# Threshold attention and mixer on one core: half of the weight tiles of six pairs transposed by TensorE, the DMA engines in the planner's model, last-row sums through SyncE's queue

## The chip, the core and the metric

The kernel runs on one core of one Trainium2 chip. A core has five engines with an instruction queue each: TensorE (PE, with its weight loads shown apart as PEld), VectorE (DVE), ScalarE (ACT), GpSimd (POOL) and SyncE (SP, which here only issues DMAs). They meet through semaphores. Sixteen DMA engines move data for all queues. The metric is the device time of one execution in microseconds (us).

## What is computed

The reference, cut to what matters (8 batches, 8 heads, 576 rows, head size 64; model size 512, hidden size 2048, rank 32):

```python
scores = scale * np.matmul(q, k.transpose(0, 1, 3, 2))
thresh = np.max(scores, axis=-1, keepdims=True) - tau
scores = np.where(scores >= thresh, scores, -1000000000.0)
scores = scores - np.max(scores, axis=-1, keepdims=True)
attn = np.exp(scores)
attn = attn / (np.sum(attn, axis=-1, keepdims=True) + 1e-09)
a = np.matmul(attn, v)                      # per batch and head
x = a.transpose(0, 2, 1, 3).reshape(B, S, H * D)
h = x.transpose(0, 2, 1) @ U @ V            # low-rank mixing of the rows
u = x + h.transpose(0, 2, 1)
out = u + np.maximum(u @ w_ch1, 0.0) @ w_ch2
```

Everything comes and goes as float32.

## The kernel before, in words

**Pairs and steps.** The 64 heads are taken as 32 pairs of two heads (four pairs a batch). A pair has five score steps, one for each tile of 128 rows of its 576 rows, so there are 160 steps; the fifth tile has 64 rows for each head, and both heads share one tile of 128 partitions. Per pair the work is:

- twelve loads of q, k and v issued by GpSimd (L271), two pairs ahead; TensorE turns q and k (L315, L330) and ScalarE copies them out (L323, L338);
- per step the scores by TensorE into the two PSUM tiles `scores0` and `scores1` (L380; L387 for the fifth), one for each head. VectorE negates and stores them with their row minimum (L400), ScalarE makes the threshold (L412) and the exponentials (L419), VectorE selects and multiplies (L427), which leaves a weight tile in one of eight buffers `w_ring` and the row sums in `d_ring`. The next step's scores wait for both L400 of the step before;
- the transpose of every weight tile by a DMA that SyncE issues (L441, eight in a pair; L444, two of half size for the fifth tile), from `w_ring` into `wT`. A buffer of `w_ring` is used again by the eighth tile after;
- the last-row sums: the sums of the fifth tile's second head lie on other partitions than the reciprocal needs, and GpSimd moves them by one tiny DMA in even batches (L457) and by two, the second waiting for the first, in odd ones (L459, L460). VectorE then takes the reciprocals (`rec`, L495 and L497);
- the product with v by TensorE (L476, two halves of 20 matmuls, called AV here), which waits for all of the pair's `wT`; the copy out (L489), the turn back (L504 to L508, called back), the scaling into `x` by VectorE (L521, L525), the low-rank product (L544, L559, L562), the sum u (L570, L574) and the turn of u (L594, L598).

After four pairs the batch has its mixer: 32 groups of four matmuls with W1 (L637, called p1 here), the ReLU on ScalarE (L647), 8 to 10 groups of eight matmuls with W2 (L663), the final sum (L676) and the stores (L689 to L693). W1 and W2 come in sixteen DMAs by GpSimd (L720, L723), one released at every second score step from the seventh on.

**The order.** Class `Order` writes the program. Each piece of work is a task with an engine, a cost in us, tasks that it waits for, and a number of the four shared PSUM banks. `run` keeps a clock for each engine and again and again takes the task that can start first; of those of one engine that could start within 0.15 us of the first, it takes the one whose `rank` is lowest (time when it was ready plus its `off`, and for the mixer a due step `when`). A task with a `lag` counts as done that long after its engine is free: 3.0 us for a load, 2.5 us for the sums, 4.5 us for a transpose in the first eight pairs and 2.8 us later. Where TensorE would wait over 0.45 us by this clock, it puts in matmuls on a constant tile (`fill`, L218), 0.22 us each. On the chip each engine runs its list in the written order and waits at whatever is not ready.

## Time and profile before

| | |
|---|---|
| median of 3 runs | 708.54 us (706.43 to 714.72) |
| the profiled execution, its own time | 708.51 us |
| its span, first to last instruction | 706.7 us |
| mean granted TensorE clock | 0.982 |
| busy | PE 677.4 us, DVE 513.1, ACT 480.3, POOL 377.5 |
| moved by DMA | 90.29 MB in 220172 packets |

How to read the views: the page gives each engine's busy time and, in 40 equal slices, its busy tenths, with the granted clock (PEclk) and the mean busy share of the sixteen DMA engines. The windows view gives the same for chosen stretches, the busy us of PE, PEld, DVE, ACT and POOL with the number of instructions behind each, then clock, DMA share (over 1 where several packets of an engine overlap) and GB/s. A row of the timeline is: start, duration, engine, line, operation, output and input, shapes, count, and in brackets the idle time of that engine just before and what ended it. Matmuls overlap, so the time from one start to the next is a little less than the duration.

### The profile page before, as it was taken

The page shows a single profiled execution, that of the slowest core. Times are in us where ns is not written, and L with a number is a line of the kernel's source. Part 1 is how long each engine was busy: PE and PEld are TensorE (multiplying, and loading weights), DVE is VectorE, ACT ScalarE, POOL GpSimd, SP SyncE. Part 2 cuts the span into 40 slices and gives each one's busy share as a digit, 9 for nine tenths or more (in the row PEclk, how much of TensorE's full clock was granted, in tenths as well). Part 3 has the DMA queues.
Part 4 walks back from the last instruction along what each step waited for, and adds up shares of the span by engine and source line. Part 5 has one row for each costly group of instructions (what it writes and reads, how often), then busy time and mean ns, then how long its engine had stood idle before and what let it go on. Part 6 is the DMA issues. An engine that isn't in the chain of part 4 may idle for free. (4 is left out here: it accounts for less than half of the span.)

```text
span 706.7 us, 15090 instructions
## 1 busy us (share of the span) xinstructions
PE 677.4 (96%) x5172; PEld 412.7 (58%) x5172; DVE 513.1 (73%) x1371; ACT 480.3 (68%) x1106; POOL 377.5 (53%) x591
## 2 busy tenths in 40 slices
PE   9997998879999999999999999999999999999994
PEld 4454555546666666656666666656666665656662
DVE  4889697568788879678788879678788878683201
ACT  5567575657778777767778777767777777765540
POOL 9967738466665466646655466646655461211111
PEclk9999998989999999999999999999999999999998
DMA  6899999978777777677776777677867775461212
GB/s 140 164 154 157 166 169 186 168 125 141 120 145 128 133 138 143 129 148 117 133 144 129 132 136 148 124 139 110 162 135 128 133 137 94 86 115 34 45 30 45
DMA packets 220172, 90.29 MB, mean 128 GB/s; under 512 B 205632, under 2 KB 210704, under 8 KB 220096
## 3 DMA queue, kind: packets, MB, share of 16 engines
q1 hardware_dynamic: 195504, 47.46, 43.7%
q0 software_dynamic: 23712, 41.66, 29.1%
q8 instruction: 41, 0.67, 0.4%
q10 hardware_dynamic: 880, 0.21, 0.1%
q14 instruction: 35, 0.29, 0.1%
HBM read 36.86 MB, written 9.44 MB: 66 GB/s over the span
## 5 line engine op out<-in xcount | busy, mean ns | idle before, releaser
L419 ACT ACTIVATE e_sb<-s_sb,m 128x576 bf16<-128x576 f32 x288 | 220.7, 766 | 71.2 <-DVE s_sb L400 69.1
L427 DVE SCALAR_TENSOR_TENSOR w_ring<-s_sb,thr,e_sb 128x576 bf16<-128x576 f32 x288 | 227.7, 820 | 41.9 <-ACT thr L412 25.8
L400 DVE TENSOR_SCALAR_CACHE_REDUCE s_sb<-scores 128x576 f32<-128x576 f32 x288 | 207.0, 751 | 54.6 <-PE scores L380 28.8
L380 PE MATMUL scores<-qkT 64*128 64x288 f32 x1024 | 168.4, 434 | 9.6 <-DVE s_sb L400 9.2
L637 PE MATMUL bank<-uT,W1b 128*128 128x288 bf16 x1024 | 141.0, 288 | 0.7 <-ACT uT L613 0.3
L663 PE MATMUL bank<-W2b,R 128*128 128x512 bf16 x576 | 135.5, 380 | 0.0
L647 ACT ACTIVATE R<-bank 128x288 bf16<-128x288 f32 x256 | 97.2, 403 | 51.4 <-PE bank L637 46.3
L637 PEld LDWEIGHTS <-W1b 128*128 128x128 bf16 x1024 | 95.7, 98 | 50.3 <-issue 24.4
L380 PEld LDWEIGHTS scores<-qkT 64*128 64x128 f32 x1024 | 95.5, 188 | 46.2 <-DVE s_sb L400 19.3
L476 PE MATMUL bank<-wT,vh 128*64 128x288 bf16 (+1 forms) x1280 | 100.7, 296 | 7.3 <-DMA wT<-w_ring 7.3
L271 POOL DMA_DIRECT2D qkraw<-in_q_dram x125 | 82.4, 677 | 38.1 <-PE bank L330 33.5
L353 POOL TENSOR_TENSOR vh<-vraw,vh 128x512 bf16<-128x512 f32 x64 | 51.5, 823 | 92.9 <-ACT vh L349 60.0
L663 PEld LDWEIGHTS <-R 128*128 128x128 bf16 x576 | 53.2, 98 | 66.1 <-issue 12.4
L271 POOL DMA_DIRECT2D vraw<-in_v_dram x128 | 84.5, 674 | 10.1 <-POOL vh L353 7.1
L476 PEld LDWEIGHTS <-vh 128*64 128x64 bf16 (+1 forms) x1280 | 62.9, 110 | 43.6 <-issue 28.3
L271 POOL DMA_DIRECT2D qkraw<-in_k_dram x125 | 81.4, 674 | 4.5 <-DMA vraw<-in_v_dram 2.6
L412 ACT ACTIVATE thr<-m,tau_t 128x2 f32<-128x2 f32 (+1 forms) x160 | 45.3, 283 | 22.5 <-DVE s_sb L400 22.3
L676 DVE TENSOR_TENSOR o<-bank,x 128x512 f32<-128x512 f32 x36 | 24.7, 687 | 44.1 <-PE bank L663 44.0
L689 POOL DMA_DIRECT2D out_dram<-o x32 | 17.8, 556 | 61.0 <-DVE o L676 50.7
L489 ACT COPY xT<-bank 128x288 f32<-128x288 f32 x64 | 24.5, 390 | 31.7 <-PE bank L476 31.3
L387 PE MATMUL scores<-qkT 64*64 64x288 f32 x256 | 39.7, 413 | 0.3 <-DVE s_sb L400 0.3
L323 ACT COPY qkT<-bank 128x512 f32<-128x512 f32 x64 | 35.6, 576 | 5.8 <-PE bank L315 5.3
(67 smaller groups left out, 567.4 us busy)
## 6 DMA issues: line engine op xcount, KB each, us to landing
out_dram<-o POOLq DMA_DIRECT2D x72, 128.0 KB, 3.5
vraw<-in_v_dram POOLq DMA_DIRECT2D x64, 80.0 KB, 2.8
wT<-w_ring SPq DMA_TRANSPOSE x320, 3.7
qkraw<-in_k_dram POOLq DMA_DIRECT2D x63, 80.0 KB, 3.7
qkraw<-in_q_dram POOLq DMA_DIRECT2D x62, 80.0 KB, 3.5
vraw<-in_v_dram POOLq DMA_DIRECT2D x64, 64.0 KB, 2.9
qkraw<-in_q_dram POOLq DMA_DIRECT2D x63, 64.0 KB, 3.4
qkraw<-in_k_dram POOLq DMA_DIRECT2D x62, 64.0 KB, 3.5
```

Source lines behind the costliest of these rows:

```text
L271: queue.dma_start(raw[part, to, j, :], src[:, of, j, :])
L353: nc.gpsimd.tensor_tensor(out=pr.vh[0:part, ts, 1, :, :], in0=pr.vraw[0:part, ts, :, :], in1=pr.vh[0:part, ts, 0, :, :], op=ALU.subtract)
L380: nc.tensor.matmul(sct[j][:, c, 0:HC], qT[hs, i * P:(i + 1) * P], kT[hs, c * HC:(c + 1) * HC], start=True, stop=True)
L387: nc.tensor.matmul(one[hs, c, 0:HC], qT[hs, 512:S], kT[hs, c * HC:(c + 1) * HC], start=True, stop=True)
L400: nc.vector.tensor_scalar(out=s_sb.rearrange("p (a c) -> p a c", a=2), in0=pair_bank[x][:, :, 0:HC], scalar1=-scale, scalar2=None, op0=ALU ...
L412: nc.scalar.activation(out=st["thr"][:, 0:nx], in_=st["m"][:, 0:nx], func=ACT.Identity, bias=tau_t[:, 0:1], scale=1.0)
L419: nc.scalar.activation(out=st["e", x], in_=st["s", x], func=ACT.Exp, bias=st["m"][:, x:x + 1], scale=-1.0)
L427: nc.vector.scalar_tensor_tensor(out=w_ring[r][:, 0:S], in0=st["s", x], scalar=st["thr"][:, x:x + 1], in1=st["e", x], op0=ALU.is_le, op1=A ...
L476: nc.tensor.matmul(av[64 * j:64 * j + 64, 0:HC], pr.vh[0:nk, kt, part, j, :], pr.wT[0:nk, kt, j, c * HC:(c + 1) * HC], start=(kt == 0 and ...
L637: nc.tensor.matmul(bank[t.got[0]][:, 0:HC], W1b[:, dt, ft * P:(ft + 1) * P], bt.uT[:, dt, c * HC:(c + 1) * HC], start=(dt == 0), stop=(dt ...
L647: nc.scalar.activation(out=R2[:, ft, lo:lo + HC], in_=bank[t.got[0]][:, 0:HC], func=ACT.Relu)
L663: nc.tensor.matmul(ch, R2[:, ft, lo:lo + P], W2b[:, ft, :], start=(ft == 0), stop=(ft == 15))
```

## The change

Four things are changed.

- **Half of the weight tiles in the first six pairs.** For the second head's tile of steps one to four of a pair (`x == 1`, 24 tiles in all) TensorE makes the transpose: five transposes of 128x128 into one shared PSUM bank, and one copy by ScalarE from the bank into `wT`. The other 40 DMA transposes of these pairs stay, and so do all of the later pairs.
- **Last-row sums.** The fifth tile's two heads swap their partition halves in odd batches, so that one DMA does in every pair; SyncE issues it, behind the fifth tile's two transposes.
- **DMA in the model.** Loads, transposes, sums, stores and weights get a cost `dma`; the planner adds them up in one running clock `moved` for all DMA engines, and a transfer counts as done 1.2 us after its turn. This replaces the fixed lags.
- **Patience.** VectorE's choice is among the tasks that could start within 0.45 us of the first, in place of 0.15.

All of the last two acts through the order alone: nothing of it is computed on the chip.

```diff
--- before.py
+++ after.py
@@ -22,6 +22,7 @@
 NT = 5
 NPAIR = H // 2
 NP = B * NPAIR
+EARLY = 6
 
 
 
@@ -43,14 +44,15 @@
 
 
 class Task:
-    __slots__ = ("engine", "cost", "fn", "deps", "off", "banks", "frees", "lag", "kind", "when",
+    __slots__ = ("engine", "cost", "fn", "deps", "off", "banks", "frees", "lag", "kind", "when", "dma",
                  "left", "after", "ready", "end", "got")
 
     def __init__(self, engine, cost, fn, deps=(), off=0.0, banks=0, frees=(), lag=0.0, kind=None,
-                 when=None):
+                 when=None, dma=0.0):
         self.engine, self.cost, self.fn = engine, cost, fn
         self.deps = [d for d in deps if d is not None]
         self.off, self.banks, self.frees, self.lag, self.kind = off, banks, frees, lag, kind
+        self.dma = dma
         self.when = when
         self.after, self.ready, self.end, self.got = [], 0.0, None, []
 
@@ -59,6 +61,7 @@
 
 
     SIGNAL = (0.25, 0.18, 0.15, 0.2, 0.1)
+    PATIENCE = (0.15, 0.45, 0.15, 0.15, 0.15)
     SWITCH = 0.05
 
     def __init__(self, nbanks, filler):
@@ -81,6 +84,7 @@
         last = [0.0] * self.nbanks
         kind = None
         steps = 0
+        moved = 0.0
 
         def rank(c):
             s, t = c
@@ -103,7 +107,7 @@
                 if not cands:
                     continue
                 first = min(s for s, _ in cands)
-                s, t = min((c for c in cands if c[0] <= first + 0.15), key=rank)
+                s, t = min((c for c in cands if c[0] <= first + self.PATIENCE[e]), key=rank)
                 if best is None or s < best[0]:
                     best = (s, t)
             assert best, "no task can start"
@@ -126,13 +130,16 @@
                 last[n] = NEVER
             at[e] = s + t.cost
             t.end = at[e] + t.lag
+            if t.dma:
+                moved = max(moved, at[e] + 0.6) + t.dma
+                t.end = moved + 1.2
             for f in t.frees:
                 for n in f.got:
                     last[n] = t.end + self.SIGNAL[e]
             t.fn(t)
             steps += t.kind == "S"
             for a in t.after:
-                a.ready = max(a.ready, t.end + (self.SIGNAL[e] if a.engine != e or t.lag else 0.0))
+                a.ready = max(a.ready, t.end + (self.SIGNAL[e] if a.engine != e or t.dma else 0.0))
                 a.left -= 1
                 if not a.left:
                     ready[a.engine].append(a)
@@ -270,7 +277,7 @@
                 src = {"q": qv, "k": kv, "v": vv}[kind]
                 queue.dma_start(raw[part, to, j, :], src[:, of, j, :])
 
-            return add(e, 0.7, fn, deps, lag=3.0, off=0.0 if p else -9.0)
+            return add(e, 0.7, fn, deps, dma=0.4, off=0.0 if p else -9.0)
 
         lo, hi = slice(0, HB), slice(HB, P)
         loads = {"q": [], "k": [], "v": []}
@@ -367,6 +374,13 @@
         pr = pairs[p]
         n = step[0]
         step[0] += 1
+
+        def half(j):
+
+
+            h = j ^ pr.batch.odd
+            return slice(64 * h, 64 * h + 64)
+
         nx = 2 if i < 4 else 1
         st = {}
 
@@ -384,7 +398,7 @@
                 for c in range(2):
                     for j in range(2):
                         hs = slice(64 * j, 64 * j + 64)
-                        nc.tensor.matmul(one[hs, c, 0:HC], qT[hs, 512:S],
+                        nc.tensor.matmul(one[half(j), c, 0:HC], qT[hs, 512:S],
                                          kT[hs, c * HC:(c + 1) * HC], start=True, stop=True)
             st["m"] = small.tile([P, 2], FP32, name="m", tag="m")
             st["thr"] = small.tile([P, 2], FP32, name="thr", tag="thr")
@@ -433,33 +447,52 @@
                 VEC, 0.77, select, [ex, thr, got("wT", tiles[0] - NW), got("rec", p - 4)],
                 off=-1.0)
 
-            def turn(_, x=x, r=tiles[0] % NW):
+            def new_wT():
                 if pr.wT is None:
                     pr.wT = wtpool.tile([P, NT, 2, S], BF16, name="wT", tag="wT")
+
+            def turn(_, x=x, r=tiles[0] % NW):
+                new_wT()
                 w_sb = w_ring[r]
                 if i < 4:
                     nc.sync.dma_start_transpose(pr.wT[:, :, x, i * P:(i + 1) * P], w_sb[:, :])
                 else:
                     for j in range(2):
-                        nc.sync.dma_start_transpose(pr.wT[:, :, j, 512:S],
-                                                    w_sb[64 * j:64 * j + 64, :])
-
-            done["wT", tiles[0]] = t = add(SP, 1.2 * (1 if i < 4 else 2), turn,
-                                           [sel, got("AV", p - 2, 0), got("AV", p - 2, 1)],
-                                           lag=2.8 if p > 7 else 4.5)
+                        nc.sync.dma_start_transpose(pr.wT[:, :, j, 512:S], w_sb[half(j), :])
+
+            def turn_pe(t, r=tiles[0] % NW):
+                ps = bank[t.got[0]][:, 0:320].bitcast(BF16)
+                for kt in range(NT):
+                    nc.tensor.transpose(ps[:, kt * P:(kt + 1) * P],
+                                        w_ring[r][:, kt * P:(kt + 1) * P], identb)
+
+            before = [sel, got("AV", p - 2, 0), got("AV", p - 2, 1)]
+            if x == 1 and p < EARLY:
+                t = done["wT", tiles[0]] = add(PE, 0.4, turn_pe, before, off=-1.0, banks=1,
+                                               kind="wT")
+
+                def copy_w(_, x=x, t=t):
+                    new_wT()
+                    nc.scalar.copy(
+                        out=pr.wT[:, :, x, i * P:(i + 1) * P],
+                        in_=bank[t.got[0]][:, 0:320].bitcast(BF16).rearrange(
+                            "p (k r) -> p k r", k=NT))
+
+                t = add(SCA, 0.68, copy_w, [t], off=-1.0, frees=[t])
+            elif i < 4:
+                t = done["wT", tiles[0]] = add(SP, 1.2, turn, before, dma=1.0)
+            else:
+                t = done["wT", tiles[0]] = add(SP, 2.4, turn, before, dma=1.0)
             done.setdefault(("wTs", p), []).append(t)
             tiles[0] += 1
             done["den", p] = sel
         if i == 4:
 
             def sums(_):
-                if pr.b % 2 == 0:
-                    nc.gpsimd.dma_start(pr.den[0:HB, 4, 1:2], pr.den[HB:P, 4, 0:1])
-                else:
-                    nc.gpsimd.dma_start(pr.den[HB:P, 4, 1:2], pr.den[HB:P, 4, 0:1])
-                    nc.gpsimd.dma_start(pr.den[HB:P, 4, 0:1], pr.den[0:HB, 4, 0:1])
-
-            done["den", p] = add(POOL, 1.1, sums, [done["den", p]], lag=2.5)
+                to, of = half(0), half(1)
+                nc.sync.dma_start(pr.den[to, 4, 1:2], pr.den[of, 4, 0:1])
+
+            done["den", p] = add(SP, 0.6, sums, [done["den", p]], dma=0.1)
 
 
     def value_tasks(p):
@@ -692,7 +725,7 @@
                     for e in (bt.even, bt):
                         nc.gpsimd.dma_start(ov[e.b, :, 4, :], o[e.h4, :])
 
-            outs.append(add(POOL, 1.15, send, [t], off=2.0, lag=2.5))
+            outs.append(add(POOL, 1.15, send, [t], off=2.0, dma=1.4))
             outs.pop(0)
         done["r4", b] = relus[1] + relus[0]
 
@@ -728,7 +761,7 @@
 
         def piece(fn, cost, to):
             nonlocal n
-            t = gate[n] = add(POOL, cost, fn, [], off=2.0, lag=5.0)
+            t = gate[n] = add(POOL, cost, fn, [], off=2.0, dma=2.7 if n > 7 else 0.5)
             to.append(t)
             n += 2
 
```

How this moves instructions is shown at three places (names: `w_ring_80` is a buffer with its number, `wT` the transposed weights, `d_ring_96` the sums of a pair; of the changed kernel the line numbers are its own, so that L441 and L476 are other lines in the two).

**SyncE's queue, third pair's end to fourth pair's end.** Before:

```order
L444 DMA_TRANSPOSE wT<-w_ring_80 128x5x64 x2
L441 DMA_TRANSPOSE wT<-w_ring_81 128x5x128
L441 DMA_TRANSPOSE wT<-w_ring_82 128x5x128
L441 DMA_TRANSPOSE wT<-w_ring_83 128x5x128
L441 DMA_TRANSPOSE wT<-w_ring_84 128x5x128
L441 DMA_TRANSPOSE wT<-w_ring_85 128x5x128
L441 DMA_TRANSPOSE wT<-w_ring_78 128x5x128
L441 DMA_TRANSPOSE wT<-w_ring_79 128x5x128
L441 DMA_TRANSPOSE wT<-w_ring_80 128x5x128
L444 DMA_TRANSPOSE wT<-w_ring_81 128x5x64 x2
```

And with the change:

```order
L461 DMA_TRANSPOSE wT<-w_ring_80 128x5x64 x2
L493 DMA d_ring_96<-d_ring_96 64x1
L458 DMA_TRANSPOSE wT<-w_ring_81 128x5x128
L458 DMA_TRANSPOSE wT<-w_ring_83 128x5x128
L458 DMA_TRANSPOSE wT<-w_ring_85 128x5x128
L458 DMA_TRANSPOSE wT<-w_ring_79 128x5x128
L461 DMA_TRANSPOSE wT<-w_ring_81 128x5x64 x2
L493 DMA d_ring_97<-d_ring_97 64x1
```

Ten transposes a pair became six, and the sums' DMA stands in this queue.

**ScalarE, second and third step of the fifth pair** (42nd to 44th exponential). Before:

```order
L419 ACTIVATE e_sb<-s_sb,m 128x576
L534 CAST xb<-x 128x512
L535 CAST xb<-x_765 64x128
L419 ACTIVATE e_sb<-s_sb,m 128x576
L412 ACTIVATE thr<-m,tau_t 128x2
L419 ACTIVATE e_sb<-s_sb,m 128x576
L550 CAST tt<-bank_157 32x128
```

And with the change:

```order
L433 ACTIVATE e_sb<-s_sb,m 128x576
L567 CAST xb<-x 128x512
L568 CAST xb<-x_591 64x128
L476 COPY wT<-bank_156 128x5x128
L433 ACTIVATE e_sb<-s_sb,m 128x576
L426 ACTIVATE thr<-m,tau_t 128x2
L433 ACTIVATE e_sb<-s_sb,m 128x576
L583 CAST tt<-bank_155 32x128
L476 COPY wT<-bank_157 128x5x128
```

One copy of a transposed tile stands between the exponentials in every step.

**VectorE, after the last select of the seventh pair** (the ninth of its selects, into `d_ring_96`). Before, the pair's reciprocal stands five instructions behind it:

```order
L427 SCALAR_TENSOR_TENSOR w_ring_84,d_ring_96<-s_sb,thr,e_sb 128x576
L400 TENSOR_SCALAR s_sb,m<-scores_153 128x576
L400 TENSOR_SCALAR s_sb,m<-scores_154 128x576
L427 SCALAR_TENSOR_TENSOR w_ring_85,d_ring_97<-s_sb,thr,e_sb 128x576
L427 SCALAR_TENSOR_TENSOR w_ring_78,d_ring_97<-s_sb,thr,e_sb 128x576
L495 TENSOR_SCALAR rec<-d_ring_96 128x10
L497 RECIPROCAL rec<-rec 128x10
```

With the change the reciprocal at this place is that of the pair before:

```order
L441 SCALAR_TENSOR_TENSOR w_ring_83,d_ring_96<-s_sb,thr,e_sb 128x576
L414 TENSOR_SCALAR s_sb,m<-scores_153 128x576
L414 TENSOR_SCALAR s_sb,m<-scores_154 128x576
L441 SCALAR_TENSOR_TENSOR w_ring_78,d_ring_97<-s_sb,thr,e_sb 128x576
L528 TENSOR_SCALAR rec<-d_ring_95 128x10
L530 RECIPROCAL rec<-rec 128x10
```

The seventh pair's own reciprocal now stands twenty instructions behind its last select, in place of five. In the same way those of the fifth, sixth and eighth pair moved from 19, 15 and 11 instructions behind to 28, 26 and 22; from the eleventh pair on they stand between one place earlier and seven later than before.

On TensorE the change adds 120 transposes and takes 50 of the 108 fills out, 48 of them before the 33rd score step and two near the end. Up to that step TensorE has otherwise the same work in both orders but for one back and two p1, which come after it now.

## Prediction

> **What bounds the kernel now.** I read the page first, then the windows, then the timelines of the stretch where TensorE is not full.
>
> ```profile
> span 706.7 us, 15090 instructions
> PE 677.4 (96%) x5172; PEld 412.7 (58%) x5172; DVE 513.1 (73%) x1371; ACT 480.3 (68%) x1106; POOL 377.5 (53%) x591
> PE   9997998879999999999999999999999999999994
> DMA  6899999978777777677776777677867775461212
> ```
>
> The span is 706.7 us and the execution's own time 708.51, so 1.8 us lie around the span; the median of the runs is the same to 0.03 us. TensorE is full from the tenth slice (a slice is 17.7 us) to the end. Only before that are there holes, and there the DMA engines show nines. The windows give the holes a size.
>
> ```profile
> 20.00:40.00 20.00, 18.70 (x135) 10.26 (x133) 17.97 (x51) 12.54 (x26) 17.41 (x27) 1.00 0.94 163
> 40.00:60.00 20.00, 19.40 (x142) 11.46 (x140) 17.70 (x51) 13.99 (x33) 15.45 (x24) 1.00 1.10 153
> 60.00:80.00 20.00, 14.83 (x111) 8.72 (x112) 13.14 (x37) 12.10 (x27) 13.93 (x23) 0.91 1.21 166
> 120.00:140.00 20.00, 17.09 (x134) 11.24 (x133) 13.99 (x38) 14.07 (x37) 12.04 (x19) 0.91 1.07 176
> 140.00:160.00 20.00, 16.45 (x120) 10.26 (x121) 11.89 (x32) 11.37 (x28) 11.75 (x17) 0.83 0.80 122
> 20.00:165.00 145.00, 127.04 (x916) 75.94 (x913) 112.59 (x308) 92.89 (x208) 99.66 (x151) 0.93 1.06 159
> 200.00:250.00 50.00, 50.00 (x396) 31.55 (x393) 40.84 (x111) 38.91 (x92) 25.20 (x40) 1.00 0.75 130
> ```
>
> There are two regimes. From 165 us on TensorE is busy 50.00 of 50 at clock 1.00: there only its own work counts. From 20 to 165 us it idles 145 - 127.04 = 18.0 us, and its clock of 0.93 costs at most 0.07 x 145 = 10.2 us more: 28 us can be had at all. Up to 60 us, where nothing is late, VectorE (17.97 and 17.70 of 20) sets the pace and fills pad TensorE. The DMA share is 1.06 there against 0.75 later. What is late is in the timelines.
>
> ```profile
> 8.29 1.24 PE L380 MATMUL scores<-qkT 64*128 64x288 f32 x8
> 42.46 2.12 PE L218 MATMUL bank<-idle 128*128 128x512 bf16 x9
> 64.88 1.24 PE L380 MATMUL scores<-qkT 64*128 64x288 f32 x8
> 71.17 2.74 PE L476 MATMUL bank<-wT,vh 128*64 128x288 bf16 x19 [2.99 <-DMA wT<-w_ring]
> 107.89 2.65 PE L476 MATMUL bank<-wT,vh 128*64 128x288 bf16 x20 [1.77 <-DMA wT<-w_ring]
> 120.23 1.24 PE L380 MATMUL scores<-qkT 64*128 64x288 f32 x8
> 134.52 1.24 PE L380 MATMUL scores<-qkT 64*128 64x288 f32 x8 [2.81 <-DVE s_sb L400]
> 146.76 2.96 PE L380 MATMUL scores<-qkT 64*128 64x288 f32 x8 [3.55 <-DVE s_sb L400]
> 110.04 0.17 DVE L495 TENSOR_SCALAR rec<-d_ring 128x10 f32<-128x10 f32 x1 [4.72 <-DMA d_ring<-d_ring]
> 131.34 0.74 DVE L495 TENSOR_SCALAR rec<-d_ring 128x10 f32<-128x10 f32 x1 [4.09 <-DMA d_ring<-d_ring]
> 145.41 0.42 DVE L495 TENSOR_SCALAR rec<-d_ring 128x10 f32<-128x10 f32 x1 [5.72 <-DMA d_ring<-d_ring]
> 107.44 0.55 POOL L460 DMA_DIRECT2D d_ring<-d_ring x1 [9.25 <-DMA d_ring<-d_ring]
> ```
>
> Two kinds of DMA end the long waits. AV waits for transposes (at 71 and 108 us). And VectorE, which runs in order, stands at a reciprocal until the last-row sums have landed: 4.72, 4.09 and 5.72 us. Scores queue behind it, so TensorE's 2.81 and 3.55 us, put down to L400, have the reciprocal as their cause. After each long hole the clock falls, and the next matmuls take twice their time (2.96 us in place of 1.24). The DMA view, over the stretches 40 to 160 and 200 to 600 us, and the SyncE queue say why:
>
> ```profile
> wT<-w_ring SPq DMA_TRANSPOSE x61, 6.3
> wT<-w_ring SPq DMA_TRANSPOSE x203, 3.5
> q1 hardware_dynamic: 195504, 47.46, 43.7%
> L441 SPq DMA_TRANSPOSE wT<-w_ring x44: 1199/1248/5024, 40.0 to 148.7; - x44
> d_ring<-d_ring POOLq DMA_DIRECT2D x10, 0.2 KB, 4.5
> ```
>
> A transpose lands after 6.3 us early and 3.5 later; the tiny sums take 4.5 early, and in odd batches two go one after the other. SyncE needs 1.25 us to issue a transpose, so ten a pair take 12.5 us, of the 15.7 us that five steps of 3.14 us last (below).
>
> **The change, part by part.** The sum has two pieces: when the 33rd score step starts (at 120.23 us before), and what follows it. I cut there because by that step both orders have done the same TensorE work but for one back and two p1, and because from there on there are mixer groups to run.
>
> *Up to the 33rd step.* Queue q1 was busy 43.7% of 706.7 us for 256 whole and 64 half transposes: 309 / 288 = 1.07 us of all sixteen engines for a whole one. The 24 that go take 25.7 us off the 1.06 x 145 = 154 us of that stretch, and 30 us (24 x 1.25) off SyncE's queue; a pair then takes 6 x 1.25 = 7.5 us there, and about 0.7 for the sums. TensorE waited 7.3 us for transposes in all (first row below), a quarter of either, and I take these waits as gone. The reciprocal of the fifth pair stands 28 VectorE instructions behind its last select in place of 19, the sixth 26 for 15, the seventh 20 for 5: at the 112.59 / 308 = 0.37 us a record of the 20 to 165 row (a select or a minimum makes two records, so 0.73 us) the 9 to 15 more instructions are some 6 to 11 us more room, against waits of 4.09 to 5.72 us. So the pace should be that of the quiet stretch: from 8.29 to 64.88 us lie 18 steps, 3.14 us each. Added to it are
>
> - 24 x 5 transposes on TensorE. Nearest are the four of L594, below: 0.10 us each with their tail, so 12 us at most, 10 by the gaps between starts. They take the place of 48 fills of 2.12 / 9 = 0.235 us, 11.3 us; TensorE's load stays, and VectorE's pace covers it;
> - 24 copies on ScalarE. Nearest are L610 with 512 columns and L419 with 576 (rows below): by 640 / 512 x 0.575 one takes 0.72 us; lower bound 0.58, upper 0.85. That is 17.3 us over 32 steps, 0.54 a step. ScalarE's 12.54 and 13.99 of 20 become about 17, under VectorE's 17.7 to 18. Hidden as long as VectorE leads; with the cover gone they cost up to 17.3 us. Queued behind a copy are exponentials, and the selects wait for these.
>
> ```profile
> PE bank L476 <- DMA wT<-w_ring: 7.3, 4, 3.0
> 63.09 0.40 PE L594 MATMUL bank<-identb,ub 128*128 128x128 bf16 x4 [0.44 <-ACT ub L581]
> 63.42 1.53 PE L476 MATMUL bank<-wT,vh 128*64 128x288 bf16 x20
> L610 ACT COPY uT<-bank 128x512 bf16<-128x512 bf16 x32 | 18.4, 575 | 2.3 <-PE bank L598 2.2
> L419 ACT ACTIVATE e_sb<-s_sb,m 128x576 bf16<-128x576 f32 x288 | 220.7, 766 | 71.2 <-DVE s_sb L400 69.1
> 118.06 0.66 PE L504 MATMUL bank<-ident,xT 128*128 128x128 f32 x4
> 119.16 1.14 PE L637 MATMUL bank<-uT,W1b 128*128 128x288 bf16 x8 [0.33 <-ACT uT L613]
> 655.10 0.59 PE L218 MATMUL bank<-idle 128*128 128x512 bf16 x2
> ```
>
> I take 3.2 us a step, a little over the quiet 3.14 for the fuller ScalarE: 8.29 + 32 x 3.2 = 110.7 us, 9.5 earlier than before.
>
> *After it.* Before, 706.7 - 120.2 = 586.5 us followed. One back (0.6) and two p1 (1.0) come over and two fills (0.5) drop out: 587.6. In this are waits and lost clock from 120 to 160 us: 2.91 + 3.55 idle, and at most 0.09 x 20 + 0.17 x 20 = 5.2 of clock, 11.7 together, all behind late reciprocals. I take 9 of it as won; the sums of these pairs no longer come in a chain of two, and the seventh pair's ten transposes are back, which is why I don't take all.
>
> The rest of the sums' move I cost at nothing. SyncE's next transposes are queued behind that DMA; it needs the same select as the two half transposes ahead of it, so it waits for nothing new. In the steady part it stands behind the two halves' issue, and so comes up to 2 x 1.25 = 2.5 us later than GpSimd's did; a pair takes about 20 us there, so VectorE might wait 6 us in 50, and it has 50 - 40.84 = 9 free, while TensorE runs on mixer work. With that cover gone it would cost up to 2.5 us a pair. GpSimd's waits of up to 9.25 us go, and its loads come earlier.
>
> *The clock under transposes.* In the 40 to 60 us window the clock is 1.00 with turns of q, k and rows among TensorE's work and fills beside them. [...] No run here shows a stretch of transposes alone.
>
> Sum: 110.7 + 587.6 - 9 + 1.8 = 691.1 us.
>
> **The rivals.**
>
> *Late transfers come back once the six pairs are over.* From the seventh pair all transposes are DMAs again while the last weight pieces still come. For it: the 120 to 140 us window has a DMA share of 1.07, and those pairs were where the reciprocal waited. Against: its later place. Then nothing of the 9 us is won: 700.1 us.
>
> *The copies lie on the path.* For it: ScalarE ends 69.1 us of waits at L419 for VectorE, so the two run in a close chain. Against: its load stays below VectorE's. All 17.3 us on the path, at 3.14 us a step: 8.29 + 100.6 + 17.3 = 126.2, and the time 706.6 us, no change.
>
> *The change does not relieve the DMA engines.* Weight pieces and loads take the room that the transposes leave; steps start where they did and all waits stay: 120.2 + 587.6 + 1.8 = 709.6 us. Against it stands the 25.7 us of transfer time that is really gone.
>
> *The clock falls: slower.* The planner pads only gaps over 0.45 us by its own clock, and 48 fills go. If the transposes or small gaps leave TensorE too idle, it runs at half clock. The work of the first 32 steps without fills is some 80 us by the shown durations (32 scores of 1.24, 10 AV of 1.53, 12 us of new transposes, and the turns of q, k and rows). With 70% of it at half clock it takes 80 x 1.7 = 136 us: the 33rd step starts at 144.3, and the time is 144.3 + 587.6 - 9 + 1.8 = 724.7 us. It makes the kernel slower by 1% from about 60% on. Against: up to 60 us the clock was 1.00, and it fell only after holes of 1.8 us and more.
>
> **How the numbers follow.** The forecast, 691 us, gets 0.72 (its own range 686 to 698: 3.14 us a step and all 11.7 won give 686.5; 3.3 and 5 won give 698.3); late transfers again 0.11 (700), copies on the path 0.07, no relief 0.04, the clock 0.06. A measurement of this kernel tells about 1% from no change, here 7 us. Faster are the forecast and three quarters of the first rival, 0.80; within 1% the rest of it, the copies and no relief, 0.14; slower 0.06. If every hole of 20 to 165 us went and the fills taken (50 x 0.235 = 11.8) made up for the transposes, 708.5 - 28.2 = 680.3 would be left, which no case should pass; the range is 681 to 703.
>
> **What would show it.** Right: the 33rd scores start at 107 to 114 us; rows of AV waiting for wT and of rec waiting for d_ring above 2 us are gone before 160 us; the clock is 1.00 from 20 to 160 us; the copies take about 0.72 us and landings of transposes are nearer 4 than 6.3 us there; from 200 us on all is as before, only shifted. Wrong: scores later than 118 us, with ScalarE above VectorE in busy time (copies), with a clock under 0.95 (gate), or with wT landing after 6 us still (no relief); or a 33rd step in time and then waits at rec.

## The result and the profile after

The changed kernel takes **684.34 us** (median of 4 runs, 683.56 to 685.97) against 709.81 (4 runs, 706.43 to 714.72): a ratio of 0.9639, 95% interval 0.9576 to 0.9702. The forecast was 691 with a range of 681 to 703. The profiled execution took 685.97 us, 1.8 of it around the span.

The page of the changed kernel, its first lines and two of its strips:

```profile
span 684.2 us, 15117 instructions
PE 660.6 (97%) x5186; PEld 408.7 (60%) x5242; DVE 517.1 (76%) x1371; ACT 492.4 (72%) x1130; POOL 354.9 (52%) x543
PE   8997999999999999999999999999999999999995
DMA  5679998976876778487868677677966586452112
```

The holes in TensorE's strip end in the fourth slice now, not in the ninth. TensorE's records sum to 16.8 us less although 120 transposes came in: fewer of its matmuls run at half clock (6.8 us at clock 0.50 between 9 and 165 us, 20.5 before), and 50 fills are gone. Part of the 16.8 us is no gain, as 56 matmuls are missing from this trace (5186 records for 5242 weight loads). The windows of the changed kernel (busy us of PE, PEld, DVE, ACT, POOL with counts; clock; DMA share; GB/s):

```profile
20.00:165.00 145.00, 135.46 (x1104) 84.95 (x1111) 130.07 (x346) 118.89 (x261) 103.62 (x153) 0.98 0.90 149
40.00:60.00 20.00, 16.80 (x149) 11.23 (x148) 18.96 (x50) 16.71 (x36) 17.11 (x26) 1.00 0.87 131
60.00:80.00 20.00, 17.68 (x138) 11.13 (x139) 17.67 (x47) 15.32 (x33) 17.05 (x26) 0.83 1.04 172
120.00:140.00 20.00, 19.60 (x167) 12.85 (x164) 15.70 (x44) 17.18 (x42) 10.18 (x15) 1.00 0.99 153
140.00:160.00 20.00, 19.79 (x153) 11.44 (x153) 16.07 (x45) 13.47 (x32) 10.99 (x16) 1.00 0.74 142
```

The reader is to see three things. From 120 us on TensorE is full at clock 1.00, where it had 17.09 and 16.45 of 20 at 0.91 and 0.83. From 40 to 60 us it is less full than before (16.80 for 19.40): the fills are gone and VectorE with 18.96 of 20 sets the pace. And one clock fall is left, from 62.44 to 69.27 us. In the 3.4 us ahead of it TensorE idles 1.70 us: behind ScalarE's copy of a turned q or k (0.89 us), and in the first half of a new wait for a select. Both stand in the timeline of TensorE beside two score steps:

```profile
59.91 0.54 PE L577 MATMUL bank<-xb,Ub 128*32 128x128 bf16 x5 [0.89 <-ACT qkT L330]
63.14 0.71 PE L466 MATMUL bank<-identb,w_ring 128*128 128x128 bf16 x5 [1.52 <-DVE w_ring L441]
110.44 1.24 PE L394 MATMUL scores<-qkT 64*128 64x288 f32 x8
302.64 1.24 PE L394 MATMUL scores<-qkT 64*128 64x288 f32 x8
673.75 2.97 PE L696 MATMUL bank<-W2b,R 128*128 128x512 bf16 x13
```

At 63.14 TensorE has stood 1.52 us at a transpose whose weight tile VectorE has not selected yet. This execution is the slowest of the four, with a mean clock of 0.992; the two fastest have 0.997 and 0.998, as the kernels below whose traces show no fall ahead of the last matmuls (0.996 and 0.997). The third and fourth row are the 33rd and the 81st score step, the last one the last matmuls. The 81st (first step of the fifth batch) is a fair second cut, for by then both orders have done the same TensorE work but for the fills and the new transposes; at steps between, one order may be a product with v or some groups of W1 ahead. The same points before (the 33rd is in the prediction):

```profile
321.07 1.24 PE L380 MATMUL scores<-qkT 64*128 64x288 f32 x8
693.83 4.05 PE L663 MATMUL bank<-W2b,R 128*128 128x512 bf16 x18
```

| stretch, us | before | after | difference | predicted |
|---|---|---|---|---|
| to the 33rd step | 120.2 | 110.4 | -9.8 | -9.5 |
| 33rd to 81st step | 200.8 | 192.2 | -8.6 | -9, and +1.1 for |
| 81st step to the end of the last matmul | 376.8 | 374.1 | -2.7 | all that follows |
| from there to the span's end | 8.9 | 7.5 | -1.4 | 0 |
| span | 706.7 | 684.2 | -22.5 | -17.4 |

The DMA view of the changed kernel, 40 to 160 us, and one row of the groups:

```profile
wT<-w_ring SPq DMA_TRANSPOSE x52, 4.3
d_ring<-d_ring SPq DMA_DIRECT2D x7, 0.2 KB, 3.1
```

```profile
L476 ACT COPY wT<-bank 128x640 bf16<-128x640 bf16 x24 | 16.2, 685 | 3.0 <-PE bank L466 3.0
```

Transposes land after 4.3 us (before 6.3), the sums after 3.1 (before 4.5), and a copy of a turned tile takes 0.685 us.

### The profile page after: what moved, and what is told of

It reads as the page before. It is cut to its first block, busy times and chain, and to the rows that moved or that the text cites. A ratio compares the mean times of both kernels' runs of the same rounds, so it can differ in the third digit from the quotient of the medians.

```text
span 684.2 us, 15117 instructions
## 1 busy us (share of the span) xinstructions
PE 660.6 (97%) x5186; PEld 408.7 (60%) x5242; DVE 517.1 (76%) x1371; ACT 492.4 (72%) x1130; POOL 354.9 (52%) x543
## 4 chain that ended last, share of the span: by engine, by line
PE 69%; issue 1%; ACT 0%; DVE 0%; POOL 0%; POOLq 0%; DVEq 0%
PE bank L670 17%; PE bank L696 16%; PE scores L394 14%; PE bank L509 9%; PE scores L401 3%; PE bank L322 3%; PE bank L537 2%; PE bank L577 2%; PE bank L592 1%; PE bank L627 1%; PE bank L337 0%; PE bank L595 0%; PE bank L631 0%; PE bank L539 0%; PE bank L541 0%
## 5 line engine op out<-in xcount | busy, mean ns | idle before, releaser
L441 DVE SCALAR_TENSOR_TENSOR w_ring<-s_sb,thr,e_sb 128x576 bf16<-128x576 f32 x288 | 230.9, 831 | 19.9 <-ACT thr L426 11.5
L394 PE MATMUL scores<-qkT 64*128 64x288 f32 x1024 | 165.3, 431 | 2.8 <-DVE s_sb L414 2.7
L696 PE MATMUL bank<-W2b,R 128*128 128x512 bf16 x525 | 129.6, 379 | 3.6 <-issue 1.4
L394 PEld LDWEIGHTS scores<-qkT 64*128 64x128 f32 x1024 | 92.9, 187 | 39.7 <-issue 10.4
L360 POOL TENSOR_TENSOR vh<-vraw,vh 128x512 bf16<-128x512 f32 x64 | 53.8, 858 | 95.0 <-ACT vh L356 54.7
L509 PE MATMUL bank<-wT,vh 128*64 128x288 bf16 (+1 forms) x1280 | 97.1, 290 | 0.0
L509 PEld LDWEIGHTS <-vh 128*64 128x64 bf16 (+1 forms) x1280 | 61.5, 109 | 34.6 <-issue 29.4
L322 PE MATMUL bank<-ident,qkraw 128*128 128x128 f32 x256 | 36.1, 276 | 1.6 <-DMA qkraw<-in_q_dram 1.1
```

The source lines that it names most:

```text
L322: nc.tensor.transpose(bank[t.got[0]][:, i * P:(i + 1) * P], pr.qkraw[:, t0 + i, :, :], ident)
L360: nc.gpsimd.tensor_tensor(out=pr.vh[0:part, ts, 1, :, :], in0=pr.vraw[0:part, ts, :, :], in1=pr.vh[0:part, ts, 0, :, :], op=ALU.subtract)
L394: nc.tensor.matmul(sct[j][:, c, 0:HC], qT[hs, i * P:(i + 1) * P], kT[hs, c * HC:(c + 1) * HC], start=True, stop=True)
L441: nc.vector.scalar_tensor_tensor(out=w_ring[r][:, 0:S], in0=st["s", x], scalar=st["thr"][:, x:x + 1], in1=st["e", x], op0=ALU.is_le, op1=A ...
L509: nc.tensor.matmul(av[64 * j:64 * j + 64, 0:HC], pr.vh[0:nk, kt, part, j, :], pr.wT[0:nk, kt, j, c * HC:(c + 1) * HC], start=(kt == 0 and ...
L696: nc.tensor.matmul(ch, R2[:, ft, lo:lo + P], W2b[:, ft, :], start=(ft == 0), stop=(ft == 15))
```

## The experiments

The change has three parts that can be taken apart: the **turns** by TensorE, the **sums** by one DMA, and the **planner** (DMA model and patience, which act through the order alone). Two theories were set against each other. *Load*: the early pairs are slow because the DMA engines are crowded, so the turns bring the gain. *Sums*: the two chained sums DMAs of odd batches make the reciprocal late and hold the queue that issues them, so the sums' move does.

**Each part alone and each left out.** Three edits of the changed kernel, which are combined. Without the turns:

```diff
-EARLY = 6
+EARLY = 0
```

Without the sums' move (the chain of before is back):

```diff
-            h = j ^ pr.batch.odd
+            h = j
...
-                nc.sync.dma_start(pr.den[to, 4, 1:2], pr.den[of, 4, 0:1])
+                if pr.b % 2 == 0:
+                    nc.gpsimd.dma_start(pr.den[0:HB, 4, 1:2], pr.den[HB:P, 4, 0:1])
+                else:
+                    nc.gpsimd.dma_start(pr.den[HB:P, 4, 1:2], pr.den[HB:P, 4, 0:1])
+                    nc.gpsimd.dma_start(pr.den[HB:P, 4, 0:1], pr.den[0:HB, 4, 0:1])
```

Without the planner's part (the fixed lags of before are back in all tasks):

```diff
-    PATIENCE = (0.15, 0.45, 0.15, 0.15, 0.15)
+    PATIENCE = (0.15, 0.15, 0.15, 0.15, 0.15)
...
-                t = done["wT", tiles[0]] = add(SP, 1.2, turn, before, dma=1.0)
+                t = done["wT", tiles[0]] = add(SP, 1.2, turn, before,
+                                               lag=2.8 if p > 7 else 4.5)
...
```

Sums and planner, no turns:

> The changed kernel with no transposes on TensorE (EARLY = 0): one DMA for the sums, the new planner and its patience stay. Load theory (the 24 DMA transposes taken off the DMA engines and SyncE's queue brought the first 33 steps forward, the single sums' DMA and the later reciprocal cured the waits after them): the 33rd scores start at about 119 us again, transposes land after 6 us in 40 to 160 us, no long wait at a reciprocal: about 696 us. Planner rival (the order alone did it): 684 to 688 us. Turns rival (the 24 transposes did all of it): 706 to 710 us.

Turns and planner, sums as before:

> The changed kernel with the last-row sums as before, one GpSimd DMA in even batches and a chain of two in odd ones, costed by the new planner. Load theory: with 24 transposes fewer the sums land sooner, but the chain of two still makes one or two waits of 2 to 4 us in pairs 5 to 7: 687 to 691 us. Turns rival and planner rival both: 683 to 686 us, as the changed kernel.

Turns and sums, planner as before:

> The changed kernel's operations (24 transposes on TensorE, one SyncE DMA for the sums) in an order made with the fixed lags and the patience of before. Load theory: 33rd scores at 110 to 113 us, reciprocals of pairs 6 to 8 stand close behind their selects again and wait 1 to 3 us each: 686 to 692 us. Turns rival: 684 to 686 us. Planner rival: 700 to 708 us.

Turns alone:

> The kernel before with the 24 transposes on TensorE and nothing else: sums by GpSimd, fixed lags and patience of before. Load theory: 33rd scores at 110 to 114 us, but the waits at the reciprocals of pairs 5 to 7 stay in part: 693 to 700 us. Turns rival: 684 to 687 us. Planner rival: 703 to 710 us.

Sums alone:

> The kernel before with the last-row sums by one SyncE DMA and nothing else: all transposes by DMA, fixed lags and patience of before. Load theory: the DMA engines and SyncE's queue are as full as before and the reciprocals stand close behind the selects, so AV waits for transposes and reciprocals wait for sums as before, less the chain of two: 701 to 707 us. Sums rival (the chain of two was the trouble): 694 to 699 us.

Planner alone:

> The kernel before with the new planner (DMA in its model, patience) and nothing else: all transposes by DMA, sums by GpSimd. With one DMA for the sums the same planner gave 697 us. Load theory: reciprocals stand late, so the waits at them go, but the first steps stay slow: 697 to 702 us. Sums rival (without the single DMA the planner can do nothing): 705 to 710 us.

Measured, with the 33rd and the 81st step and the time from there to the end of the last matmul, in the profiled execution (that of the planner alone lies 2.3 us above its median, that of sums and planner 3.3). Each ratio is to executions of before that were taken beside the kernel, with medians of 708.54 to 709.81 us:

| kernel | median us | ratio (95%) | 33rd | 81st | rest |
|---|---|---|---|---|---|
| before | 709.65 | | 120.2 | 321.1 | 376.8 |
| planner alone | 707.64 | 0.9947 (0.9907 to 0.9987) | 126.1 | 321.6 | 377.3 |
| turns alone | 698.38 | 0.9858 (0.9787 to 0.9929) | 112.5 | 307.5 | 379.9 |
| sums and planner | 697.08 | 0.9846 (0.9785 to 0.9908) | 130.5 | 317.3 | 374.1 |
| sums alone | 692.86 | 0.9759 (0.9719 to 0.9800) | 121.7 | 308.1 | 375.5 |
| turns and sums | 688.89 | 0.9741 (0.9657 to 0.9824) | 109.2 | 305.3 | 375.3 |
| turns and planner | 688.79 | 0.9731 (0.9672 to 0.9789) | 110.1 | 302.6 | 375.5 |
| all three | 684.34 | 0.9639 (0.9576 to 0.9702) | 110.4 | 302.6 | 374.1 |

The expectations for sums alone and for the planner alone failed. By the load theory the sums alone were to bring 3 to 9 us; they brought 16.8, the largest single part, and more than the sums theory gave them. The planner alone brought 2.0 by the medians and 3.8 by the ratio (its ten runs spread from 699.38 to 712.86), where the load theory had 7 to 12. For turns and planner the time came as the load theory had it, but not the waits that it named: VectorE has none at a reciprocal before 165 us. And the parts don't add: 2 + 10 + 17 is 29, the whole is 25.

The columns say who does what. The **33rd step** comes early in the four kernels with turns (109 to 113 us) and in none without (120 to 131; the 130.5 is no delay, since that order has 76 matmuls of W1 ahead of the step for 8 before, 0.14 us each): that stretch belongs to the turns, as the load theory has it. Whether they help there by freeing the DMA engines or by shortening SyncE's queue of transposes is not shown, as every kernel with turns does both. At the **81st step**, where the work is equal, turns alone have won 13.6 us, sums alone 13.0, and both together 15.8 on the old planner's order: each cures most of what the other cures. With the planner it is another story: beside the turns it adds 5 (9.6 by the medians of the whole), beside the sums it takes 9 away (4.2 by the medians). In its order without turns VectorE's selects wait 6.6 us for buffers whose transposes aren't done, which no other of these orders shows in that size; whether that is all of it was not tried. The **rest** is 374.1 to 375.5 in the kernels with one DMA, 375.5 to 379.9 in those with the chain.

So the load theory's forecast holds for the turns, and the sums theory for something that the load theory prices at nothing. What that is, two more kernels show.

**The chain by itself.** Sums alone is also another order, since GpSimd lost a task. Two kernels part the chain from the issuer and the order. The first is the kernel before with the halves swapped, so that GpSimd issues one DMA; every engine's list is that of before, but for the sums:

```diff
-                if pr.b % 2 == 0:
...
+                to, of = half(0), half(1)
+                nc.gpsimd.dma_start(pr.den[to, 4, 1:2], pr.den[of, 4, 0:1])
```

> The kernel before, in its own order of instructions on every engine, with one thing changed: in odd batches the halves of the fifth tile are swapped, so that GpSimd issues one sums DMA in place of a chain of two. Theory of the chain (GpSimd's queue stands behind the second DMA of the chain, 9.25, 3.92 and 6.31 us in pairs five to eight, and loads and weight pieces with it): most of what the sums' move alone brought (16.8 us) comes from here, 693 to 699 us, and GpSimd has no wait above 3 us for its own sums DMA. Theory of the issuer and the order (it matters that SyncE issues it, or that the planner writes another order when GpSimd has no such task): 704 to 712 us, with the reciprocals at 110 to 146 us waiting as before.

The second is sums alone with the chain put back, issued by SyncE (`h = j`, and the if and else of the second edit with `nc.sync` in place of `nc.gpsimd`):

> The order of instructions of the kernel with the sums' move alone (692.9 us), but the heads are not swapped: in odd batches SyncE issues the two chained DMAs, the second waiting for the first. Theory of the chain: the wait of 4 to 9 us now stands in SyncE's queue, ahead of the next pair's transposes, and AV and the selects wait for those: 700 to 720 us. Theory of the issuer and the order: the chain itself matters little, 691 to 697 us.

Measured: the chain taken out of before, 697.84 us, 0.9840 (0.9797 to 0.9883); the chain put into sums alone, 708.77 us, 1.0001 (0.9963 to 1.0039). Both came where the chain theory had them: in one order of instructions the chain costs 11, in the other 16 us. What is left between GpSimd and SyncE with one DMA each, 5 us, is at the edge of the two intervals (0.9797 and 0.9800 touch) and holds another order too: it stays open. By the 81st step the first has won 10.0 us and the second lost 12.3, behind it 1.5 and 2.7 more: later odd batches pay for the chain too, though less. How much of the loss comes by the late reciprocal, and how much by what stands behind the chain's second DMA in its queue, these two kernels don't part.

Where most of it is lost shows in the windows from 120 to 160 us. Before, one DMA by GpSimd, sums alone, and sums alone with the chain, in this order:

```profile
120.00:160.00 40.00, 33.55 (x252) 21.50 (x251) 25.88 (x70) 25.44 (x63) 23.79 (x36) 0.87 0.93 149
```

```profile
120.00:160.00 40.00, 38.31 (x300) 24.09 (x298) 31.64 (x86) 30.20 (x74) 23.33 (x34) 0.96 1.02 156
```

```profile
120.00:160.00 40.00, 38.66 (x316) 24.30 (x315) 35.51 (x98) 31.17 (x77) 23.40 (x35) 1.00 1.11 171
```

```profile
120.00:160.00 40.00, 33.63 (x266) 21.50 (x265) 29.38 (x81) 27.86 (x67) 21.93 (x33) 0.91 0.90 144
```

With the chain TensorE loses 5 us of 40 and then clock, whoever issues it. Without it the DMA engines are busier (1.02 and 1.11 for 0.93 and 0.90), and it is the faster for that: the crowd is not what costs here. The row that carries the loss is the reciprocal. In the kernel with the chain on SyncE, VectorE and TensorE:

```profile
151.12 0.17 DVE L533 TENSOR_SCALAR rec<-d_ring 128x10 f32<-128x10 f32 x1 [7.22 <-DMA d_ring<-d_ring]
153.70 2.19 PE L401 MATMUL scores<-qkT 64*64 64x288 f32 x8 [4.34 <-DVE s_sb L414]
```

and with one DMA by GpSimd, where before had 4.09 and 5.72 us in this stretch:

```profile
137.90 0.17 DVE L530 TENSOR_SCALAR rec<-d_ring 128x10 f32<-128x10 f32 x1 [2.79 <-DMA d_ring<-d_ring]
139.00 2.30 PE L394 MATMUL scores<-qkT 64*128 64x288 f32 x8 [1.59 <-DVE s_sb L414]
```

Sums alone has no wait of a reciprocal above 1 us between 118 and 162 us; it has one of 6.84 us at 75.41, in the even batch, where no chain ever was, and beside it TensorE waits for transposes:

```profile
71.97 0.45 PE L511 MATMUL bank<-wT,vh 128*64 128x288 bf16 x1 [4.22 <-DMA wT<-w_ring]
75.24 2.50 PE L511 MATMUL bank<-wT,vh 128*64 128x288 bf16 x17 [2.83 <-DMA wT<-w_ring]
75.41 0.19 DVE L530 TENSOR_SCALAR rec<-d_ring 128x10 f32<-128x10 f32 x1 [6.84 <-DMA d_ring<-d_ring]
```

With these waits its 33rd step is not early.

**Whether the copies are hidden.** Each of the 24 copies is issued twice:

```diff
-                    nc.scalar.copy(
+                    for _ in range(2):
+                        nc.scalar.copy(
```

> The changed kernel with each of the 24 ScalarE copies of transposed tiles issued twice, the order else the same: ScalarE gets some 24 x 0.65 = 16 us more between 20 and 110 us. Theory that the copies are hidden behind VectorE's pace: 683 to 688 us. Theory that ScalarE lies in a close chain with VectorE and each copy is on the path: 695 to 701 us, and the 33rd score step starts 10 us later or more.

Measured: 690.55 us, 0.9753 (0.9693 to 0.9812), between the two theories: 6 us by the medians, 3.1 by the profiled spans, for 24 x 0.689 = 16.5 us more. The 33rd step starts at 112.78, 2.3 us later than in the changed kernel's trace, which has a clock fall ahead of it, and 4.4 later than with ten pairs (108.34, below), the same order up to there and like this one without a fall. The stretch from 20 to 110 us, of this kernel:

```profile
20.00:110.00 90.00, 77.38 (x653) 48.13 (x649) 81.20 (x216) 85.56 (x174) 71.90 (x109) 1.00 0.94 148
```

and of the changed kernel:

```profile
20.00:110.00 90.00, 81.24 (x681) 50.92 (x685) 83.99 (x222) 74.70 (x157) 75.33 (x112) 0.96 0.93 152
```

Doubled copies make ScalarE the fullest engine (85.56 of 90), and even then a part of them shows, 6 of 16.5 us by the medians. With single ones VectorE leads by 9 us: so the 16.2 us of the change should lie mostly beside it. How much of them is on the path can't be read more closely than that.

**More pairs.**

```diff
-EARLY = 6
+EARLY = 10
```

> The changed kernel with half of the weight tiles of ten pairs in place of six transposed by TensorE. Theory that from the 33rd score step on only TensorE's own work counts: 16 x 0.45 = 7 us are added to a full TensorE, and at most the one select wait is won: 686 to 692 us. Theory that the crowded DMA engines still cost time in pairs seven to ten: 676 to 682 us.

Measured: 689.50 us, 0.9725 (0.9676 to 0.9774), as the first theory had it: 5 us slower than six pairs. The window from 120 to 160 us:

```profile
120.00:160.00 40.00, 38.74 (x338) 24.82 (x335) 32.00 (x85) 32.27 (x71) 21.12 (x31) 1.00 0.50 104
```

The DMA share falls from 0.87 to 0.50 there and nothing is won by it: TensorE was full (39.39 of 40 at clock 1.00 in the changed kernel), and 16 x 5 more transposes are its own work. From the 33rd to the 81st step it takes 197.3 us for 192.2: 5.1 us, or 0.32 for each tile of five. Up to the 33rd step its order is that of the changed kernel, but without the clock fall:

```profile
108.34 1.24 PE L394 MATMUL scores<-qkT 64*128 64x288 f32 x8
```

So the fall at 62 us made the changed kernel's trace some 2 us late at this step.

**The fills and the clock.** Two edits of the changed kernel: only the first 15 of 58 fills are kept; and every fill is three transposes in place of one matmul.

```diff
+        filled[0] += 1
+        if filled[0] <= 15:
+            nc.tensor.matmul(bank[n], idle[:, 0:P], idle, start=True, stop=True)
```

> The changed kernel in the same order with 41 of its 58 or so fills left out, all but the first 15: TensorE idles where they stood. [...]

```diff
-        nc.tensor.matmul(bank[n], idle[:, 0:P], idle, start=True, stop=True)
+        ps = bank[n][:, 0:192].bitcast(BF16)
+        for i in range(3):
+            nc.tensor.transpose(ps[:, i * P:(i + 1) * P], idle[:, i * P:(i + 1) * P], identb)
```

> The changed kernel with every fill made of three bf16 transposes of the idle tile in place of one matmul, of about the same length. Load theory: they count as busy, clock 1.00 from 5 us on but for the one fall that the changed kernel has too, 683 to 687 us. [...]

Few fills: 687.69 us, 0.9684 (0.9635 to 0.9733), with three clock falls (0.51, 0.51 and 0.50 from 17.50 to 24.50, 31.30 to 38.20 and 48.40 to 55.20 us) and the 33rd step at 111.14. So the remaining fills are worth some 3 us by the medians (the intervals overlap), and a kernel that runs some 20 us at half clock ahead of the 33rd step comes only 2.8 us later there than ten pairs without a fall: behind the falls VectorE sets the pace (18.91, 19.55 and 18.68 of 20 us from 60 to 120), and TensorE makes most of its loss up. Transposes as fills: 683.99 us, 0.9627 (0.9586 to 0.9667), the same as matmuls. Its first rows on TensorE:

```profile
2.79 3.61 PE L227 MATMUL bank<-identb,idle 128*128 128x128 bf16 x36 [2.79 <-DVE identb L175]
6.24 1.04 PE L324 MATMUL bank<-ident,qkraw 128*128 128x128 f32 x8
22.52 1.63 PE L324 MATMUL bank<-ident,qkraw 128*128 128x128 f32 x8
```

The eight turns of q and k at 6.24 us take 1.04 us, the time at full clock (1.00 from 5.80 to 8.00 us; 1.06 us in the changed kernel, behind matmuls), with nothing but 36 transposes ahead of them. The same eight at 22.52, largely at half clock (0.50 from 22.90 to 26.31 us), take 1.63.

## Why the prediction was right, and where it was not

- **The start of the 33rd step, 110.7: right in cause, and close in size by some luck.** It came at 110.44, but behind a clock fall that the sum doesn't have; without a fall the same order has it at 108.34, which is (108.34 - 8.27) / 32 = 3.13 us a step, the quiet pace. The 3.2 that was taken for the fuller ScalarE does not show, and the fall made up for it. AV's waits for transposes are gone before 165 us, and the step is early in all kernels with turns and in no other. The 24 transposes cost TensorE nothing that shows, as VectorE's pace covers them.
- **The copies, 0.72 us: right** (0.685). **Hidden: borne out as far as it can be read**, with little to spare, as a second set already shows in part.
- **What follows, 9 of 11.7 us won and 1.1 taken over: right.** -7.9 was forecast, -8.6 measured by the 81st step. The rival that late transfers return did not come about: from 110 to 165 us transposes landed after 3.6 us in the median, and taking still more off the DMA engines made it slower.
- **"The rest of the sums' move I cost at nothing": the step that failed.** The end of the chain of two was named, but only as a reason beside the reciprocal's later place, without a price of its own. Alone the sums' move is worth 16.8 us, more than the turns (10), and the chain alone costs 11 us in one order and 16 in another. On top of the other two parts it is still 4.5 us by the medians, though the intervals overlap; by the profiles it is 2.8, of which 1.4 lie between the 81st step and the last matmul, where the prediction expected everything as before, and 1.4 behind that. From the 81st step to the last matmul the whole change won 2.7 us, and the first chain kernel shows 1.5 for the chain alone in one order of instructions. The total came out near, partly by luck, because turns, later reciprocal and the end of the chain cure the same waits ahead of the 81st step: counting them once, as the sum did, was right, and giving them to the turns and the later place was one cure of two.
- **The 6 to 11 us more room for the reciprocal** did its part: turns and planner, with the chain still there, have no wait of VectorE for sums between 20 and 165 us, and are at the 81st step when all three are.
- **The clock: no fall of the kind that the slower rival wanted.** The granted clock was 0.98 from 20 to 165 us, not 1.00, with one fall, of 6.8 us, behind the two waits at 60 to 63 us. That transposes in the place of fills cost the clock nothing was the author's estimate from a single window; the kernel whose fills are transposes bears it out: clock 1.00 at 6.24 us, behind 36 transposes alone, and one fall up to 165 us, of 3.4 us.
- **What else the sum lacked.** 1.4 us of the 5 between forecast and profile are the tail behind the last matmul: 8.9 us before, 7.5 after. It goes with the engine that issues the sums: 8.2 to 9.2 in the five kernels where GpSimd does, with the chain or without, and 7.1 to 7.5 in the nine where SyncE does. The last store lands 1.6 us after its issue either way, and the span ends 4.5 to 5.1 us after that where GpSimd issues the sums and 3.4 to 3.7 where SyncE does; why stays open.

## What to carry over

Here a tiny DMA that waited for another tiny DMA cost whoever needed it two landings, and from 40 to 160 us a landing took 3.1 us in the median after the change and 4.5 before: change which half goes where, so that one move does, before looking for bandwidth. When several parts of a change cure the same wait, measure each alone and each left out, as the sum of the single gains is not the whole and one part may look worthless beside the others. Here off-loading the queue paid as long as the engine that took the work wasn't the bound: six pairs won, ten gave 5 us back.

## What the runs showed of the hardware

Behind transposes alone TensorE came to full speed (above): the first 36 took 3.61 us, 0.10 each, and at 15.43 us of the same kernel, with the clock at 1.00, 15 took 1.00 us, 0.07 each.

The granted clock of the kernel before and of the changed one was 1.00 or 0.50, and each fall between 9 and 165 us lasted 3.41 us or twice that: 3.41, 6.83, 3.41 and 6.83 us before, 6.83 after. Cut into stretches of 3.41 us from these changes on, these two kernels and the one with transposes as fills have 123 stretches at full clock with another behind them in that time. Six were followed by half clock, with TensorE busy 0.31, 0.64, 1.23, 1.64, 1.65 and 1.71 us; of the other 117 the two emptiest have 2.05 and 2.30. In the kernel with few fills half clock followed behind 2.10, 2.11 and 2.27 us (stretches cut to some 0.2 us), so that the busy time by these records does not settle it there. The longest hole alone says less. The first row below, of the kernel before, holds one of 1.37 us and full clock followed; the second, ahead of the changed kernel's fall, none over 0.89 us:

```profile
64.07:67.49 3.42, 2.05 (x22) 1.04 (x16) 3.42 (x10) 2.85 (x7) 2.47 (x5) 1.00 1.30 173
59.03:62.44 3.41, 1.71 (x13) 0.99 (x13) 3.41 (x7) 3.41 (x8) 3.41 (x6) 1.00 1.23 220
```

And in the kernel with few fills half clock followed a stretch whose one hole is a stall of 1.31 us:

```profile
14.10:17.50 3.40, 2.09 (x17) 1.09 (x14) 2.71 (x9) 2.95 (x7) 3.40 (x7) 1.00 0.76 176
17.50:24.50 7.00, 6.66 (x31) 3.75 (x29) 5.94 (x16) 5.14 (x12) 7.00 (x11) 0.51 0.68 131
```

The prediction found falls only behind holes of 1.8 us and more. In these four kernels the longest hole does not tell a fall; the sum of the gaps in such a stretch does where it is 1.7 us or more (a fall behind each) or 1.1 us and less (behind none).
